# Loading the dense input matrix ahead of the first key piece in a decode step of sliding-window attention and a Mish layer

## The chip, the cores and the metric

The kernel runs on one core of one Trainium2 chip. The metric is the device time of one execution in microseconds. The profile is of one execution; its span, from the first to the last instruction, is a little shorter than the device time.

## The reference

A decode step for a batch of 2, one token each, width 448. The input is normalised once, and two branches are added to it.

```python
xn = layernorm(x)                                   # x: (2, 1, 448)
# attention: 16 query heads, 8 key/value heads, head size 256, last 4096 of 32768 positions
q = (xn @ wq) in 16 heads
p = softmax(q @ k[last 4096].T * 256 ** -0.5)
a = (p @ v[last 4096]) @ wo
# dense: 448 -> 1792 -> 448
h = xn @ w1 + b1
d = (h * tanh(softplus(h))) @ w2
out = x + a + d
```

All inputs are bfloat16. The keys and values of the window are 2 x 8 x 4096 x 256 numbers each, 67 MB together; with the four weight matrices 77.67 MB are read in one execution.

## The kernel before, in words

The work is written out by hand: a manual schedule keeps the instructions of each engine in the order of the program text, and the framework adds the semaphores.

**Units.** The 16 pairs of batch and key head are handled in U = 4 units of J = 4 pairs. A unit's keys come in two pieces, k(u,0) and k(u,1), its values in two pieces, v(u,0) and v(u,1). Each piece is 4096 KB: 128 partitions of 32 KB. A unit's part of the output matrix, wo(u), has 896 KB.

**The ring.** Large loads share three buffers of 32 KB per partition, handed out by `ring` (tag "kv"): wq (two halves of 1792 KB), all key and value pieces, the dense input matrix w1 (1568 KB) and the dense output matrix w2. A load into a used buffer waits until the last reader of the old content is done. All these loads are issued by SyncE, one after the other, so a load that waits holds up those behind it in the program.

**Start.** wq is loaded, then k(0,0) and k(0,1), then the bias b1. Meanwhile the layer norm is computed and the normalised input is turned into `xs`. `project()` makes the queries: 28 matmuls `q_ps` against wq, a copy, transposes, and the spread queries `qd` (its PSUM tiles share one buffer, tag "m"). w1 takes the buffer of wq once the projection has read it.

**Per unit.**
- `turns(u, i)` transposes a key piece on VectorE in 32 x 32 blocks, two instructions a piece (L269 in the profile before).
- `scores(u, i)` writes a mask into PSUM and adds 32 matmuls (L356); ScalarE takes the exponential (L364). After i = 1 VectorE transposes the weights into `p` (L367) and swaps two blocks (`swap`).
- `weigh(u)` sums the weights (`dn`, `rec`).
- `values(u, g)` multiplies a value piece by the weights, 32 matmuls (L402).
- `gather`, `finish`, `relay`, `mix_early` divide by the sum and multiply by wo.

The loop over u issues the loads k(u+1,0), v(u,0), k(u+1,1), v(u,1), wo(u) and then turns and scores of unit u+1 beside the values of unit u.

**The dense branch.** `dense_in()` makes h in PSUM in seven groups, each a bias matmul (L510) and seven matmuls with w1 as the stationary operand (L519). Its PSUM tile `h_ps` uses the same buffer (tag "m") as the projection's last tile `qr_ps`. `mish()` is one exponential on ScalarE (L533) and five small VectorE instructions (L535 to L544). Before, both stand in the text between `turns(0, 1)` and `scores(0, 1)`. The output matrix w2 comes last of all loads, in four parts, and `dense_out` adds its products to `acc`, from which `res` is copied and stored.

Of the kernel before, what the change touches and what calls it, by code (L numbers as in the profile page):

```python
# [17 lines left out]
def kernel(  # L18
# [13 lines left out]
    nc = tc.nc  # L32
    P = 128
# [24 lines left out]
    NS = 7  # L58
    HW = HqDh // 2
    NCH = HW // P  # L60
    F2 = F // 2
# [28 lines left out]
    def ring(name):  # L90
        return kv_pool.tile([P, RK * KE], BF16, tag="kv", name=name)
# [3 lines left out]
    def load_k(u, r):  # L95
        t = ring("k")
        src = kview[u][:, s0:, :].rearrange("j (c t) d -> c j (t d)", c=C)
        nc.sync.dma_start(out=t[:], in_=src[:, :, r * RK * KE : (r + 1) * RK * KE])
        k_t[u, r] = t
# [20 lines left out]
    b1_sb = consts.tile([2, F2], BF16)  # L120
# [4 lines left out]
    for lo in (0, half):  # L125
        nc.sync.dma_start(out=wq[:, lo : lo + half], in_=wq_in[:, lo : lo + half])
    wq_t = [wq[:, i * HW : (i + 1) * HW] for i in range(NS)]
    load_k(0, 0)
    load_k(0, 1)
    nc.sync.dma_start(out=b1_sb[:], in_=B_b1.rearrange("(k f) -> k f", k=2))  # L130

    ident = consts.tile([P, P], BF16)
    make_identity(nc, ident[:])
# [6 lines left out]
        out=halves[:], in_=ident[0:2, 0:2].unsqueeze(2).to_broadcast([2, 2, Bsz])  # L140
# [5 lines left out]
    for k in range(KU):  # L146
        nc.gpsimd.tensor_copy(
            out=hot[:, k, :, :, :, k],
            in_=ident[:].rearrange("p (q y) -> p y q", y=4).unsqueeze(2)
# [11 lines left out]
        out=rstd[:], in_=mv[:, 1:2], func=ACT.Sqrt, bias=eps_t[:], scale=1.0  # L161
# [4 lines left out]
        out=xn_bf[:],  # L166
# [8 lines left out]
        out=parm[:], in_=ident[:].rearrange("p (a o) -> p o a", o=2), axis=AXIS.X, op=ALU.add  # L175
# [3 lines left out]
        out=jm[:],  # L179
        in_=ident[:].rearrange("p (a j h) -> p j a h", j=J, h=rep),  # L180
# [4 lines left out]
        out=jm[:], in0=jm[:], scalar1=-1.0, scalar2=29952.0, op0=ALU.add, op1=ALU.mult  # L185
# [3 lines left out]
        out=mneg[:], in_=jm[:].unsqueeze(1).to_broadcast([P, TH * 8, J])  # L189
    )  # L190
    sel = consts.tile([P, 2, NQ], FP32)
    for x in range(2):
        for w in range(4):
# [4 lines left out]
            else:  # L198
                nc.vector.tensor_tensor(
                    out=sel[:, x, :], in0=sel[:, x, :], in1=src, op=ALU.add  # L200
# [16 lines left out]
    for odd in range(2):  # L217
        for half in range(2):
            o = (half + odd) % 2
            nc.vector.tensor_scalar(  # L220
                out=xs[:, odd::2, half * Bsz : (half + 1) * Bsz],
# [44 lines left out]
    def turns(u, i):  # L266
        t = k_t.pop((u, i))
        for r in range(RK):
            nc.vector.transpose(  # L269
                out=kt[i][:, :, r, :, :],  # L270
                in_=t[:, r * KE : (r + 1) * KE].bitcast(FP32).rearrange(
                    "p (a c j) -> p a c j", c=P // (R * J), j=J
                ),
            )

    spread = {}
    for n in range(2):
        for e in range(2):
# [3 lines left out]
                out=sp[:],  # L282
                in_=ident[:, o : o + 63 : 2].unsqueeze(1).to_broadcast([P, G, 32]),
# [3 lines left out]
    def project():  # L287
        q_ps = ps_m.tile([P, 512], FP32, tag="m", name="q_ps")
        for s in range(NS):
            for u in range(U):  # L290
                nc.tensor.matmul(  # L291
                    q_ps[32 * u : 32 * (u + 1), :],
                    lhsT=xs[:, s, :],
                    rhs=wq_t[s][:, u * 512 : (u + 1) * 512],
                    start=(s == 0),
                    stop=(s == NS - 1),
                    skip_group_check=True,
                )
        q_sb = small.tile([P, 4, P], BF16, tag="vs", name="q_sb", bufs=1)
        nc.scalar.copy(out=q_sb[:].rearrange("p a m -> p (a m)"), in_=q_ps[:])  # L300
        qt_ps = ps_m.tile([P, 4, P], BF16, tag="m", name="qt_ps")
        for a in range(4):
            nc.tensor.transpose(qt_ps[:, a, :], q_sb[:, a, :], ident[:])  # L303
        qT = consts.tile([P, 2, U, Bsz, KU, rep], BF16)
        q_v = qt_ps[:].rearrange("p (h c) (u r) -> p c u r h", c=2, u=U)
        for c in range(2):
            for b in range(Bsz):
                nc.vector.tensor_copy(  # L308
                    out=qT[:, c, :, b, :, :], in_=q_v[:, c, :, b : KU * Bsz : Bsz, :]
                )  # L310
        qr_ps = ps_m.tile([P, 2 * NB, U, NQ], FP32, tag="m", name="qr_ps")
        for n in range(NB):
            for e in range(2):
                nc.tensor.matmul(
                    qr_ps[:, 2 * n + e, :, :].rearrange("p u q -> p (u q)"),
                    lhsT=spread[n % 2, e][:].rearrange("p g a -> p (g a)"),
                    rhs=qT[:, n // 2].rearrange("p u b k h -> p (u b k h)"),
                    start=True,
                    stop=True,
                    skip_group_check=True,  # L320
                )
        for g in range(G):
            rows = slice(g * 32, (g + 1) * 32)
            nc.vector.tensor_copy(
                out=qd[rows, :, :, g, :],
                in_=qr_ps[rows].rearrange("p n u q -> p u n q"),
            )
# [47 lines left out]
    state = {}  # L375
# [119 lines left out]

    act_bf = consts.tile([P, NI, 2, Bsz], BF16)

    def load_w1():
        t = ring("w1")
        nc.sync.dma_start(  # L500
            out=t[:, 0 : NS * F2], in_=B_w1.flatten().rearrange("(p e) -> p e", p=P)
        )
        state["w1"] = t

    def dense_in():
        w1 = state.pop("w1")
        w1_v = w1[:, 0 : NS * F2].rearrange("p (s q i) -> p s i q", s=NS, i=NI)
        h_ps = ps_m.tile([P, NI, 2, Bsz], FP32, tag="m", name="h_ps")
        for i in range(NI):
            nc.tensor.matmul(  # L510
                h_ps[:, i, :, :].rearrange("p k b -> p (k b)"),
                lhsT=b1_sb[:, i::NI],
                rhs=halves[:].rearrange("p k b -> p (k b)"),
                start=True,
                stop=False,
                skip_group_check=True,
            )
            for s in range(NS):
                nc.tensor.matmul(  # L519
                    h_ps[:, i, :, :].rearrange("p k b -> p (k b)"),  # L520
                    lhsT=w1_v[:, s, i, :],
                    rhs=xs[:, s, 0 : 2 * Bsz],
                    start=False,
                    stop=(s == NS - 1),
                    skip_group_check=True,
                )
        state["h"] = h_ps

    def mish():
        h_ps = state.pop("h")  # L530
        shape = [P, NI, 2, Bsz]
        u_sb = consts.tile(shape, FP32, name="u_sb")
        nc.scalar.activation(out=u_sb[:], in_=h_ps[:], func=ACT.Exp)  # L533
        t_sb = consts.tile(shape, FP32, name="t_sb")
        nc.vector.scalar_tensor_tensor(  # L535
            out=t_sb[:], in0=u_sb[:], scalar=2.0, in1=u_sb[:], op0=ALU.add, op1=ALU.mult
        )
        den = consts.tile(shape, FP32, name="den_sb")
        nc.vector.tensor_scalar(
            out=den[:], in0=t_sb[:], scalar1=2.0, scalar2=None, op0=ALU.add  # L540
        )
        nc.vector.reciprocal(out=den[:], in_=den[:])
        nc.vector.tensor_tensor(out=t_sb[:], in0=t_sb[:], in1=den[:], op=ALU.mult)
        nc.vector.tensor_tensor(out=act_bf[:], in0=h_ps[:], in1=t_sb[:], op=ALU.mult)  # L544
# [15 lines left out]
    def dense_out(part):  # L560
        k, lo, hi = w2_parts[part]
        for i in range(lo, hi):
# [2 lines left out]
                act_bf[:, i, k, :], state["w2"][:, at : at + D], stop=(k == 1 and i == NI - 1)  # L565
            )

    load_w1()
    project()
    turns(0, 0)  # L570
    scores(0, 0)
    turns(0, 1)
    dense_in()
    mish()
    scores(0, 1)
    weigh(0)
    for u in range(U - 1):
# [77 lines left out]
```

The softmax here doesn't subtract the row's maximum and nothing guards it: scores larger than these inputs give would overflow.

## Time and profile before

| what | value |
|---|---|
| device time, median of 3 runs | 189.21 us (188.96 to 189.25) |
| span of the profiled execution | 187.2 us |
| TensorE matmul busy | 78.2 us, 42% |
| VectorE busy | 92.7 us, 50% (70.1 us of it the key transposes L269) |
| ScalarE busy | 12.6 us, 7% |
| read from HBM | 77.67 MB, 415 GB/s over the span |
| DMA queue of the loads | 97.0% of 16 engines' span |

The DMA rows of the profile give, for each of 40 slices of the span, the busy share of the core's 16 DMA engines in tenths and the rate. The chain of waits follows the work that ended last back to what released it. The timeline of the SP queue shows when a load is issued; that of an engine shows an instruction group's start, its duration, and in brackets how long the engine was idle before it and what ended that. Engine times are from the span's start.

### The profile page before, as it was taken

Reading aid. Unit: us, or ns where it says so; the run is one execution under the profiler, and the core shown is the slowest. Engines: PE = TensorE matmul, PEld = TensorE weight load, DVE = VectorE, ACT = ScalarE, POOL = GpSimd, SP = SyncE. Lnnn points to the kernel's source line nnn. Section 1 sums busy time; section 2 is a strip of 40 time slices with the busy share of each in tenths; the row PEclk is TensorE's granted clock in tenths of the full one; section 3 lists DMA queues with packets and bytes.
Section 4 is the critical chain, followed back from the end, with each engine's and each line's share of the span. In section 5 each row is a group of like instructions: output and inputs, shape, how many; then the busy total and the mean of one; then the engine's idle time right before and its main releaser. Section 6 shows DMA issues by size and latency. Waiting matters only on the chain.

```text
span 187.2 us, 1951 instructions
## 1 busy us (share of the span) xinstructions
PE 78.2 (42%) x852; PEld 35.3 (19%) x852; DVE 92.7 (50%) x94; ACT 12.6 (7%) x27; POOL 4.9 (3%) x16
## 2 busy tenths in 40 slices
PE   0453014793219200882049002870067004855684
PEld 0211001551003000440012001420022002422283
DVE  6604397984792098038930395048920593040021
ACT  3003000101000100110000100110001000120101
POOL 8100000000000000000000000000000000000000
PEclk9999999958555855698556755897557555996555
DMA  6999999999999999999999999999999999999991
GB/s 218 420 476 441 427 434 387 454 438 448 441 427 420 403 443 404 464 434 448 441 420 424 413 441 417 451 431 448 434 434 420 413 441 427 441 413 416 417 407 42
DMA packets 4195, 77.78 MB, mean 416 GB/s; under 512 B 470, under 2 KB 732, under 8 KB 1628
## 3 DMA queue, kind: packets, MB, share of 16 engines
q1 hardware_dynamic: 4184, 77.67, 97.0%
q8 instruction: 6, 0.10, 0.2%
q14 instruction: 1, 0.01, 0.0%
q10 hardware_dynamic: 4, 0.00, 0.0%
HBM read 77.67 MB, written 0.00 MB: 415 GB/s over the span
## 4 chain that ended last, share of the span: by engine, by line
DMA 62%; PE 17%; DVE 15%; issue 3%; ACT 1%; SPq 0%; DVEq 0%
DMA v<-in_A_v_cache_dram 30%; DMA k<-in_A_k_cache_dram 15%; DVE kt L269 12%; DMA w<-in_B_w_dram 11%; DMA wq<-in_A_wq_dram 6%; PE pv L402 5%; PE sc L356 3%; PE h_ps L519 2%; PE o L420 1%; DVE p L367 1%; PE acc L249 1%; PE dn L380 1%; PE q_ps L291 1%; PE o L435 1%; DVE rec L388 1%
## 5 line engine op out<-in xcount | busy, mean ns | idle before, releaser
L269 DVE STREAM_TRANSPOSE kt<-k 128x4096 f32<-128x4096 f32 x16 | 70.1, 4420 | 33.9 <-DMA k<-in_A_k_cache_dram 33.9
L402 PE MATMUL pv<-v,p 128*32 128x512 bf16 x244 | 25.5, 590 | 72.3 <-DMA v<-in_A_v_cache_dram 72.3
L356 PE MATMUL sc<-kt,qd 128*32 128x512 bf16 x256 | 20.8, 463 | 13.3 <-DVE kt L269 13.3
L402 PEld LDWEIGHTS <-p 128*32 128x32 bf16 x244 | 9.2, 133 | 86.7 <-issue 63.4
L356 PEld LDWEIGHTS <-qd 128*32 128x32 bf16 x256 | 7.4, 109 | 25.5 <-issue 20.5
L364 ACT ACTIVATE ex<-sc 128x512 bf16<-128x512 f32 x8 | 4.8, 597 | 89.6 <-PE sc L356 89.6
L447 DVE TENSOR_TENSOR oT<-o,rec 128x16 bf16<-128x16 f32 x4 | 0.7, 174 | 20.4 <-PE o L420 18.1
L367 DVE STREAM_TRANSPOSE p<-ex 128x512 bf16<-128x512 bf16 x8 | 5.2, 690 | 10.6 <-ACT ex L364 10.6
L388 DVE TENSOR_REDUCE rec<-dn 128x8 f32<-128x512 f32 x4 | 2.8, 692 | 13.5 <-PE dn L380 13.5
L414 ACT COPY vs<-pv 128x512 f32<-128x512 f32 x4 | 2.3, 585 | 56.5 <-PE pv L402 56.5
L420 PE MATMUL o<-sel,vs 128*128 128x8 f32 x32 | 5.2, 289 | 2.1 <-ACT vs L414 2.1
L482 PE MATMUL early<-wo,ox 128*2 128x448 bf16 x24 | 5.0, 352 | 1.9 <-ACT ox L473 1.9
L420 PEld LDWEIGHTS o<-sel,vs 128*128 128x128 f32 x32 | 4.8, 228 | 4.6 <-ACT vs L414 4.6
L380 PE MATMUL dn<-p,ones 128*128 128x512 bf16 x8 | 3.2, 491 | 3.8 <-DVE p L338 3.8
L291 PE MATMUL q_ps<-wq,xs 128*32 128x512 bf16 x28 | 3.8, 623 | 2.3 <-DMA wq<-in_A_wq_dram 1.9
L519 PE MATMUL h_ps<-xs,w 128*128 128x4 bf16 x49 | 3.7, 196 | 1.3 <-DMA w<-in_B_w_dram 1.3
L345 PE MATMUL sc<-mneg,ident 128*128 128x512 bf16 x8 | 4.1, 516 | 0.0
L308 DVE COPY qT<-qt_ps 128x16 bf16<-128x16 bf16 x4 | 0.4, 165 | 7.1 <-PE qt_ps L303 7.1
L212 PE MATMUL xr_ps<-ident,xrows 2*128 2x2 bf16 x7 | 1.0, 181 | 6.7 <-DVE xrows L211 6.7
L519 PEld LDWEIGHTS <-w 128*128 128x128 bf16 x49 | 3.2, 150 | 1.5 <-DMA w<-in_B_w_dram 1.4
L482 PEld LDWEIGHTS <-ox 128*2 128x2 bf16 x24 | 1.8, 83 | 4.1 <-ACT ox L473 2.2
L212 PEld LDWEIGHTS <-xrows 2*128 2x128 bf16 x7 | 0.7, 99 | 6.9 <-DVE xrows L211 6.7
(68 smaller groups left out, 44.9 us busy)
## 6 DMA issues: line engine op xcount, KB each, us to landing
k<-in_A_k_cache_dram SPq DMA_DIRECT2D x8, 4096.0 KB, 27.9
v<-in_A_v_cache_dram SPq DMA_DIRECT2D x7, 4096.0 KB, 21.3
wq<-in_A_wq_dram SPq DMA_DIRECT2D x2, 1792.0 KB, 9.2
wo<-in_A_wo_dram SPq DMA_DIRECT2D x4, 896.0 KB, 18.9
v<-in_A_v_cache_dram SPq DMA_DIRECT2D x1, 2560.0 KB
w<-in_B_w_dram SPq DMA_DIRECT2D x1, 1568.0 KB, 21.2
v<-in_A_v_cache_dram SPq DMA_DIRECT2D x1, 1024.0 KB, 22.0
w<-in_B_w_dram SPq DMA_DIRECT2D x1, 784.0 KB, 22.2
```

The source lines that it names most:

```text
L269: nc.vector.transpose(out=kt[i][:, :, r, :, :], in_=t[:, r * KE : (r + 1) * KE].bitcast(FP32).rearrange("p (a c j) -> p a c j", c=P // (R ...
L291: nc.tensor.matmul(q_ps[32 * u : 32 * (u + 1), :], lhsT=xs[:, s, :], rhs=wq_t[s][:, u * 512 : (u + 1) * 512], start=(s == 0), stop=(s == N ...
L345: nc.tensor.matmul(sc[:].rearrange("p t c m -> p (t c m)"), lhsT=ident[:], rhs=mneg[:].rearrange("p a j -> p (a j)"), start=True, stop=Fal ...
L356: nc.tensor.matmul(sc[32 * w : 32 * (w + 1)].rearrange("p t c m -> p t (c m)"), lhsT=qd[:, u, 2 * n + e, :, :].rearrange("p g q -> p (g q) ...
L364: nc.scalar.activation(out=ex[:, :, :, i, :], in_=sc[:], func=ACT.Exp, scale=scale)
L367: nc.vector.transpose(out=p_all[:, :, h * TH : (h + 1) * TH, :].rearrange("p g t q -> p t g q"), in_=ex[:, h * TH : (h + 1) * TH].rearrang ...
L380: nc.tensor.matmul(dn[:].rearrange("p a q -> p (a q)"), lhsT=ones[:], rhs=p_run[:, i].rearrange("p t q -> p (t q)"), start=(i == 0), stop= ...
L388: nc.vector.tensor_reduce(out=rec[:], in_=dn[:].rearrange("p a q -> p q a"), axis=AXIS.X, op=ALU.add)
L402: nc.tensor.matmul(pv[32 * w : 32 * (w + 1), :, :].rearrange("p x d -> p (x d)"), lhsT=p_run[:, g, 4 * a : 4 * a + 4, :].rearrange("p t q ...
L420: nc.tensor.matmul(po[:, c, :], lhsT=sb[:, x, c::2], rhs=sel[:, x, :], start=(x == 0 and c == 0), stop=(last and x == 1), skip_group_check ...
L482: nc.tensor.matmul(early[:], lhsT=ox[:, i, :], rhs=w[:, i, :], start=False, stop=(u == U - 2 and i == 7),)
L519: nc.tensor.matmul(h_ps[:, i, :, :].rearrange("p k b -> p (k b)"), lhsT=w1_v[:, s, i, :], rhs=xs[:, s, 0 : 2 * Bsz], start=False, stop=(s ...
```

## The change

The load of w1 and that of b1 move ahead of the key pieces. w1 takes a ring buffer of its own at the start instead of that of wq, and so the second key piece, k(0,1), now takes the buffer of wq and waits for the projection. `dense_in()` and `mish()` move from between `turns(0, 1)` and `scores(0, 1)` to right behind `project()`, before the first key piece is transposed. The aim is to have the dense input stage done while the first key piece is still on its way, and out of the way of unit 0's scores.

```diff
@@ start
     wq_t = [wq[:, i * HW : (i + 1) * HW] for i in range(NS)]
+    nc.sync.dma_start(out=b1_sb[:], in_=B_b1.rearrange("(k f) -> k f", k=2))
+    w1 = ring("w1")
+    nc.sync.dma_start(
+        out=w1[:, 0 : NS * F2], in_=B_w1.flatten().rearrange("(p e) -> p e", p=P)
+    )
     load_k(0, 0)
     load_k(0, 1)
-    nc.sync.dma_start(out=b1_sb[:], in_=B_b1.rearrange("(k f) -> k f", k=2))
@@ dense branch
-    def load_w1():
-        t = ring("w1")
-        nc.sync.dma_start(
-            out=t[:, 0 : NS * F2], in_=B_w1.flatten().rearrange("(p e) -> p e", p=P)
-        )
-        state["w1"] = t
-
     def dense_in():
-        w1 = state.pop("w1")
@@ order
-    load_w1()
     project()
+    dense_in()
+    mish()
     turns(0, 0)
     scores(0, 0)
     turns(0, 1)
-    dense_in()
-    mish()
     scores(0, 1)
```

## The prediction

> **What bounds the kernel now.** I read the page first: the DMA rows of its part 2 and the queues of part 3.
>
> ```profile
> DMA  6999999999999999999999999999999999999991
> GB/s 218 420 476 441 427 434 387 454 438 448 441 427 420 403 443 404 464 434 448 441 420 424 413 441 417 451 431 448 434 434 420 413 441 427 441 413 416 417 407 42
> q1 hardware_dynamic: 4184, 77.67, 97.0%
> ```
>
> 38 of 40 slices say 9, while PE is busy 42% and DVE 50%. The digits round, so I next asked for stretches (columns: PE, PEld, DVE, ACT, POOL busy, granted clock, DMA share, GB/s):
>
> ```profile
> 2.00:14.00 12.00, 5.07 (x36) 1.78 (x36) 5.32 (x30) 0.87 (x2) 3.52 (x10) 1.00 1.00 420
> 14.00:36.00 22.00, 6.07 (x56) 2.77 (x54) 15.21 (x11) 2.46 (x3) 0.00 (x0) 1.00 1.00 431
> 36.00:60.00 24.00, 13.54 (x124) 6.59 (x127) 17.07 (x16) 0.79 (x2) 0.00 (x0) 0.59 1.01 435
> 60.00:120.00 60.00, 21.03 (x218) 8.18 (x210) 29.55 (x14) 3.18 (x7) 0.00 (x0) 0.65 1.01 432
> 120.00:182.00 62.00, 30.02 (x339) 13.95 (x339) 24.37 (x22) 4.08 (x11) 0.00 (x0) 0.68 0.99 425
> ```
>
> The DMA share is 0.99 to 1.01 in every stretch from 2 to 182 us. The packet records of the trace are sharper: in each half microsecond from about 2.6 to 181.6 us, 16.0 or more of 16 engines have a packet, and the usual duration of the 1920 packets of 32768 bytes is 1213 ns. So nothing is idle where the change acts, and each byte has a fixed price: 77.67 MB at some 430 GB/s.
>
> The end of the chain of waits shows that the tail hangs on the last transfer:
>
> ```profile
> 182.01 1.98 PE acc L249 x76
> 183.99 0.02 issue
> 184.01 0.57 PE acc L249 x12
> 184.58 0.25 DVE res L621
> ```
>
> The last packets end between 182.3 and 183.9 us, depending on the engine. The 12 matmuls from 184.01 come after the last packet, then the `res` copies, then the store of the output. The change touches none of these.
>
> Last, the order at the start. The timeline of the SP queue shows when a load could be issued, that of DVE when a key piece landed:
>
> ```profile
> 1.65 1.25 SPq L98 DMA_DIRECT2D k<-in_A_k_cache_dram  x2
> 14.19 0.36 SPq L500 DMA_DIRECT2D w<-in_B_w_dram  x1
> 30.73 0.55 SPq L98 DMA_DIRECT2D k<-in_A_k_cache_dram  x1
> 39.61 0.54 SPq L106 DMA_DIRECT2D v<-in_A_v_cache_dram  x1
> 40.45 0.53 SPq L98 DMA_DIRECT2D k<-in_A_k_cache_dram  x1
> 57.45 0.54 SPq L106 DMA_DIRECT2D v<-in_A_v_cache_dram  x1
> ```
>
> ```profile
> 21.93 8.77 DVE L269 STREAM_TRANSPOSE kt<-k 128x4096 f32<-128x4096 f32 x2 [3.76 <-DMA k<-in_A_k_cache_dram]
> 31.66 8.77 DVE L269 STREAM_TRANSPOSE kt<-k 128x4096 f32<-128x4096 f32 x2 [0.95 <-DMA k<-in_A_k_cache_dram]
> 48.70 8.72 DVE L269 STREAM_TRANSPOSE kt<-k 128x4096 f32<-128x4096 f32 x2
> 65.18 8.77 DVE L269 STREAM_TRANSPOSE kt<-k 128x4096 f32<-128x4096 f32 x2 [7.76 <-DMA k<-in_A_k_cache_dram]
> ```
>
> Key piece k(0,0) landed at 21.93 and k(0,1) at 31.66: 9.73 us for 4.19 MB, or 431 GB/s. The dense matrix w1 landed at 35.36 (the chain ends its wait there), 3.70 us later. The third pair of transposes (48.70) waited for earlier DVE work and not for its data. The fourth waited 7.76 us for its data: DVE is ahead again by then.
>
> **What the Trainium skill says.** "DMA: Bandwidth & Descriptors", section Specifications, gives a fabric ceiling of 435 GB/s for a core's 16 DMA engines; the trace's 431 to 435 GB/s agree. Its section on the anatomy of one DMA says that DMA engines do not wait on semaphores: the issuing sequencer waits before dispatch, and the engines merely consume their queues. The SP rows agree: each load is issued when its ring buffer comes free, up to 21 us before its data has landed (w1: 14.19 to 35.36). So a later issue costs time only if the queue has run empty by then. "Runtime: NRT & Kernel Launch", section Instruction fetch mechanics, says that instructions are fetched in 16 KiB blocks; the six packets (0.10 MB) on queue 8 of the page agree.
>
> **The change part by part.** I follow the new order step by step, with durations from before.
>
> 1. *Bytes and packets.* The same loads with the same shapes; only the order differs: wq, b1, w1, k(0,0), k(0,1). DMA work changes by 0. b1 is two rows, 3.5 KB.
>
> 2. *Landings.* wq is still first, so it lands at 12.2 and the projection ends at 14.17 as before. w1 lands 3.70 us after wq, at 15.9. k(0,0) moves from 21.93 to 25.6 and k(0,1) from 31.66 to 35.4, where w1 landed before. The bytes ahead of k(1,0) are the same, so from there nothing is due earlier or later: k(1,0) at 35.4 + 9.7 = 45.1, v(0,0) at 55.3 (its first matmul before), k(1,1) at 65.2.
>
> 3. *dense_in and mish.* `h_ps` uses the PSUM buffer of `qr_ps`, so the first matmul waits for the `qd` copies (16.45 + 1.72 = 18.2); w1 is there. The seven groups took 35.40 to 39.58, 4.2 us, so they end at about 22.4. Queued behind them on PE is `scores(0, 0)`, which cannot go on before the first transposes of k(0,0) end (about 30). The Exp takes 0.19 us; the five DVE steps of mish took 40.35 to 41.59, 1.24 us, and end by 24.0. Queued behind them on DVE are the transposes of k(0,0), whose data comes at 25.6. The table load for Exp (1.28 us, at 14.79 before) now stands ahead of mish's Exp and still lies beside the projection's tail. All hidden: cost 0.
>
> 4. *The new wait on the ring.* Three buffers hold wq, w1 and k(0,0), so k(0,1) waits for wq's last reader: it is issued at 14.2 instead of about 2. The queue then holds the rest of w1 and all of k(0,0), to 25.6: 11 us of work. Behind k(0,1) on SP stand the other loads:
>    - k(1,0) takes w1's buffer after dense_in: 22.4 (30.73 before), needed when k(0,1) lands, 35.4.
>    - v(0,0) takes k(0,0)'s after its transposes: 25.6 + 8.8 = 34.4 (39.61 before), needed at 45.1.
>    - k(1,1) takes k(0,1)'s: 35.4 + 8.8 = 44.2 (40.45 before), needed at 55.3.
>
> 5. *The tightest place.* v(0,1) needs the transposes of k(1,0) to end. After 44.2 PE does the rest of `scores(0, 1)`: 30 matmuls, 3.15 us as at 30.76 before, or 3.9 us at the lower clock seen at 40. Exp, softmax transposes, swap, sums and reciprocal then took from 43.92 to 48.70, 4.8 us. So k(1,0)'s transposes start at 52.2 to 52.9 (48.70 before) and end 8.7 us later, at 60.9 to 61.6. v(0,1) is issued then instead of at 57.45. The queue empties at 65.2. A load's first packet came 1.0 us after its issue at the very start (0.73 to 1.74). That leaves 2.6 to 3.3 us unused.
>
> 6. *After that.* wo(0) and k(2,0) follow v(0,1) at once, as `values(0, 0)` ends near 58.9. The transposes of k(1,1) start with its landing at 65.2, since DVE is free at 61.6, and everything behind is as before. The delay of 3.7 us ends in DVE's wait of 7.76 us.
>
> Sum: 0 on the path. Forecast: 189.2 us.
>
> **The rivals.**
>
> *A bubble in the queue (slower).* Step 5 could be too hopeful: if PE runs slow, or a ring buffer is freed later than I read it, the engines idle, and idle DMA time cannot be won back. For it speaks that v(0,1)'s margin shrinks by 3.5 to 4.2 us. Against it: 2.6 us are still left, and the other margins are 11 to 13 us. If a bubble opened, I would expect 0.5 to 3.7 us (the whole shift): 189.7 to 192.9, most likely about 191.
>
> *A different tail (either side).* The engines do not end together: 182.3 to 183.9. By the packet records, a fetch on queue 8 holds the engine it falls on for 0.87 us, and the packet behind lasts 1.76 us instead of 1.21: 1.4 us together, the size of the spread. PE's instructions change places near the start, so its first fetch may come at another moment, and two fetches on one engine would add up to 1.4 us: 190.6. A better mix ends at most near the mean of the engines, about 0.6 us earlier: 188.6. Against both: the number of instructions is practically the same and the last fetches are far from the change.
>
> *Faster by freed compute.* mish leaves DVE's stretch before the transposes of k(1,0), and PE has dense_in out of its way. If the path were compute, 1.2 us of DVE or up to 4.2 us of PE could go: 188.0 to 185. Against it: the DMA share is 1.00 in that stretch, so earlier compute waits for data.
>
> **How the numbers follow.** No change 0.74; a bubble 0.09; a worse tail 0.05; a better tail 0.09; freed compute 0.03. Hence faster 0.12, same 0.74, slower 0.14. The measured runs of before spread over 0.3 us. The range runs from the best tail, 188.6, to 189.9, which takes in a small bubble or half of a bad tail.
>
> **What would show it right or wrong.** Right: a DMA share near 1.00 in every stretch from 2 to 182; k(0,0)'s transposes near 25.6 and k(0,1)'s near 35.4; dense matmuls from 18 to 22.5; the third pair of transposes at 52 to 53; v(0,1) issued near 61; the fourth pair at 65.2 as before. Step 5 is wrong if a slice near 65 us falls below 0.9 and the first `values` of v(0,1) come after 75. The whole argument is wrong if the time drops by a microsecond with all loads the same, since then the rate of the DMA engines is not fixed.

## The result, and the profile after

The changed kernel takes 190.69 us (median of 6 runs, 190.34 to 191.03) against 189.21 us (188.96 to 189.33). The ratio is 1.008, with a 95% interval from 1.0065 to 1.0095: it is 1.5 us slower. All the work that was moved is hidden, as meant. The time is lost some 40 us later, at the load v(0,1), whose place in the program the change leaves alone.

The DMA rows and the load queue of the page of the changed kernel:

```profile
DMA  6999999999999999999999999999999999999990
GB/s 216 417 426 492 417 420 417 438 431 438 445 445 438 344 419 392 470 445 424 445 424 414 438 431 419 443 438 441 431 445 424 424 407 469 417 421 399 412 389 33
q1 hardware_dynamic: 4184, 77.67, 96.8%
```

The busy row looks as before: 38 slices of 9. The row below it does not. The 14th slice (61.3 to 66.0 us) moved 344 GB/s, the slices beside it 438 and 419. Two stretches asked for on both kernels (columns as in the prediction: PE, PEld, DVE, ACT, POOL busy, clock, DMA share, GB/s) show it apart from the grid of the page. The kernel before:

```profile
44.00:60.00 16.00, 5.65 (x43) 1.80 (x46) 11.70 (x9) 0.52 (x1) 0.00 (x0) 0.59 1.00 432
62.00:70.00 8.00, 0.00 (x0) 0.00 (x0) 4.82 (x2) 0.59 (x1) 0.00 (x0) 0.63 1.02 437
```

The changed kernel:

```profile
44.00:60.00 16.00, 8.49 (x66) 2.92 (x67) 10.78 (x10) 0.60 (x1) 0.00 (x0) 0.72 1.02 442
62.00:70.00 8.00, 3.10 (x30) 1.06 (x23) 5.01 (x2) 0.60 (x1) 0.00 (x0) 0.71 1.00 392
```

Between 62 and 70 us the engines are "busy" for a share of 1.00 and move 392 GB/s instead of 437. Eight microseconds at 45 GB/s less are 0.36 MB, 0.8 us of transfer. What was issued then, by the timeline of the SP queue:

```profile
2.41 20.99 SPq L98 DMA_DIRECT2D k<-in_A_k_cache_dram  x3
35.30 0.54 SPq L106 DMA_DIRECT2D v<-in_A_v_cache_dram  x1
44.82 0.54 SPq L98 DMA_DIRECT2D k<-in_A_k_cache_dram  x1
61.73 0.54 SPq L106 DMA_DIRECT2D v<-in_A_v_cache_dram  x1
62.32 0.60 SPq L112 DMA_DIRECT2D wo<-in_A_wo_dram  x1
63.01 0.56 SPq L98 DMA_DIRECT2D k<-in_A_k_cache_dram  x1
```

The load at 61.73 is v(0,1). Its buffer came free with the third pair of transposes; the timeline of DVE:

```profile
26.50 8.77 DVE L273 STREAM_TRANSPOSE kt<-k 128x4096 f32<-128x4096 f32 x2 [2.13 <-DMA k<-in_A_k_cache_dram]
36.02 8.77 DVE L273 STREAM_TRANSPOSE kt<-k 128x4096 f32<-128x4096 f32 x2 [0.75 <-DMA k<-in_A_k_cache_dram]
52.99 8.72 DVE L273 STREAM_TRANSPOSE kt<-k 128x4096 f32<-128x4096 f32 x2
64.99 8.77 DVE L273 STREAM_TRANSPOSE kt<-k 128x4096 f32<-128x4096 f32 x2 [3.29 <-DMA k<-in_A_k_cache_dram]
```

The fourth pair starts at 64.99, as early as before (65.18): up to the landing of k(1,1) nothing is lost. The next landing is that of v(0,1), and on it waits the next group of values on PE:

```profile
76.25 3.60 PE L406 MATMUL pv<-v,p 128*32 128x512 bf16 x32 [11.16 <-DMA v<-in_A_v_cache_dram]
```

In the kernel before it started at 74.87:

```profile
74.87 3.29 PE L402 MATMUL pv<-v,p 128*32 128x512 bf16 x32 [12.98 <-DMA v<-in_A_v_cache_dram]
```

So it is 1.4 us late. The end carries the same shift (end of the chain of waits):

```profile
183.45 1.95 PE acc L253 x57
185.40 0.01 issue
185.41 0.61 PE acc L253 x12
186.01 0.25 DVE res L616
```

The last 12 matmuls come at 185.41 instead of 184.01, 1.4 us later. The groups of values in between that wait for their data start 1.2 to 1.4 us later as well.

The packet records tell what "busy at 392 GB/s" is. In the table, "engines" counts packets in flight, and the rate spreads each packet over its own duration.

```
us           before: engines, GB/s     after: engines, GB/s
62.5 - 63.0        16.0   425               15.9   429
63.0 - 63.5        16.2   423               15.3   382
63.5 - 64.0        16.0   424               13.7   281
64.0 - 64.5        16.1   425               14.0   284
64.5 - 65.0        16.1   431               15.2   300
65.0 - 65.5        16.0   433               16.1   358
66.0 - 66.5        16.0   433               16.1   398
68.0 - 68.5        16.1   435               16.0   414
69.0 - 69.5        16.1   434               16.0   429
```

The records don't name the engine, but a packet that starts where no other has just ended follows a pause. Four engines have finished k(1,1) at 62.94, 63.23, 63.46 and 63.53, and find nothing behind it. The packets after these pauses start at 63.07, 63.71, 64.62 and 64.77: 1.3 to 3.0 us after the issue of v(0,1) at 61.73. The idle time is small, about 0.2 us in the mean of the 16 engines. The larger part is in long packets: 32 KB packets of v(0,1) last up to 2.6 us instead of 1.21, and it takes until 69 us to be back at full rate. This is how the queue behaved at its very start as well: in the kernel before 183 GB/s from 2.0 to 2.5 us, 363 from 3.0 and 420 from 4.0. So for some of its engines the queue ran dry, and the whole of it ramped up a second time. Why the packets are long, no run here shows.

### The profile page after: what moved, and what is told of

Its sections match the earlier page's. It is cut to its first block, busy times and chain, and to the rows that moved or that the text cites. A ratio compares the mean times of both kernels' runs of the same rounds, so it can differ in the third digit from the quotient of the medians.

```text
span 188.6 us, 1947 instructions
## 1 busy us (share of the span) xinstructions
PE 84.0 (45%) x847; PEld 38.5 (20%) x852; DVE 93.0 (49%) x94; ACT 12.6 (7%) x27; POOL 4.6 (2%) x16
## 3 DMA queue, kind: packets, MB, share of 16 engines
q1 hardware_dynamic: 4184, 77.67, 96.8%
HBM read 77.67 MB, written 0.00 MB: 412 GB/s over the span
## 4 chain that ended last, share of the span: by engine, by line
DMA 61%; DVE 20%; PE 11%; issue 3%; SPq 1%; ACT 1%; another core or an unknown queue 1%; DVEq 0%
DMA v<-in_A_v_cache_dram 29%; DMA k<-in_A_k_cache_dram 26%; DVE kt L273 16%; DMA wq<-in_A_wq_dram 6%; PE pv L406 4%; PE sc L360 3%; DVE p L371 1%; PE acc L253 1%; PE q_ps L295 1%; PE o L424 1%; DVE rec L392 1%; ACT ex L368 1%; SPq L106 1%; PE o L439 0%
## 5 line engine op out<-in xcount | busy, mean ns | idle before, releaser
L273 DVE STREAM_TRANSPOSE kt<-k 128x4096 f32<-128x4096 f32 x16 | 70.0, 4414 | 22.8 <-DMA k<-in_A_k_cache_dram 22.8
L406 PE MATMUL pv<-v,p 128*32 128x512 bf16 x244 | 24.8, 577 | 61.0 <-DMA v<-in_A_v_cache_dram 61.0
L360 PE MATMUL sc<-kt,qd 128*32 128x512 bf16 x256 | 25.6, 537 | 18.4 <-DVE kt L273 18.4
L360 PEld LDWEIGHTS <-qd 128*32 128x32 bf16 x256 | 8.6, 123 | 33.9 <-issue 32.8
L424 PE MATMUL o<-sel,vs 128*128 128x8 f32 x32 | 7.5, 364 | 2.1 <-ACT vs L418 2.1
L424 PEld LDWEIGHTS o<-sel,vs 128*128 128x128 f32 x32 | 7.1, 326 | 5.5 <-ACT vs L418 5.5
L384 PE MATMUL dn<-p,ones 128*128 128x512 bf16 x4 | 2.0, 499 | 4.0 <-DVE p L342 3.8
L143 DVE COPY halves<-ident 2x4 bf16<-2x4 bf16 x1 | 1.9, 1912 | 1.3 <-POOL ident masks.py:199 1.3
## 6 DMA issues: line engine op xcount, KB each, us to landing
v<-in_A_v_cache_dram SPq DMA_DIRECT2D x7, 4096.0 KB, 22.4
```

The costliest lines, as they stand in the source:

```text
L273: nc.vector.transpose(out=kt[i][:, :, r, :, :], in_=t[:, r * KE : (r + 1) * KE].bitcast(FP32).rearrange("p (a c j) -> p a c j", c=P // (R ...
L360: nc.tensor.matmul(sc[32 * w : 32 * (w + 1)].rearrange("p t c m -> p t (c m)"), lhsT=qd[:, u, 2 * n + e, :, :].rearrange("p g q -> p (g q) ...
L406: nc.tensor.matmul(pv[32 * w : 32 * (w + 1), :, :].rearrange("p x d -> p (x d)"), lhsT=p_run[:, g, 4 * a : 4 * a + 4, :].rearrange("p t q ...
L424: nc.tensor.matmul(po[:, c, :], lhsT=sb[:, x, c::2], rhs=sel[:, x, :], start=(x == 0 and c == 0), stop=(last and x == 1), skip_group_check ...
```

## The experiments

Theory: v(0,1) is issued too shortly before the engines run out. Rival 1: loading the dense matrix first costs in itself (a slower start, a wider spread of the engines at the end). Rival 2: the instruction fetch that falls on 63.02 us, 0.05 us ahead of the first long packet, makes the dip; the kernel before had it at 62.03. In the expectations, lead is the time from the issue of v(0,1) to the moment at which the queue has moved as many bytes as were issued ahead of it, by the packet records: 6.04 us before, 1.94 us after. (At that moment, 63.67 us after the change, some engines are past these bytes and others not yet.)

**More bytes ahead of v(0,1).**

```diff
+        if u == 0:
+            load_wo(u)
         load_v(u, 1)
-        load_wo(u)
+        if u > 0:
+            load_wo(u)
```

> The changed kernel with one load moved: wo(0), which needs no ring buffer, is issued before v(0,1) instead of behind it, so 0.92 MB more stand in the queue while v(0,1) waits for the transposes of k(1,0). Theory (a load issued too shortly before the queue runs empty makes the engines drain and ramp up again): v(0,1) is still issued near 61.7, but the bytes ahead of it last 2.1 us longer, so its lead grows from 1.9 to about 4 us; the dip near 63 to 68 us goes away and the time is 189.2 to 189.5. Rival 1 (the early dense load costs time in another way: a slower start, a wider spread of the engines at the end): the time stays 190.4 to 191.0. Rival 2 (the instruction fetch that fell on 63.0 made the dip): the fetch stays where it is, and so do the dip and 190.7.

Measured 189.91 us (188.97 to 190.48, 22 runs), ratio to the kernel before (now 189.05 us in 49 runs) 1.0031 [1.0017, 1.0046]: about half of the loss is gone, and not all as the theory had said. The runs lie between no loss and nearly the full one. In the profiled run (189.78 us) v(0,1) was issued at 62.21 with a lead of 3.56 us, and still engines were idle from 65.07 on; the packets after a pause started at 65.6 to 66.5, 3.4 to 4.3 us after the issue. Bytes ahead help, so rival 1 alone cannot be right; but a lead of 3.6 us was not enough.

**The buffer freed earlier.** In unit 0, the transposes of k(1,0) go ahead of the softmax work on VectorE; loads as in the changed kernel.

```diff
     turns(0, 1)
+    load_k(1, 0)
+    turns(1, 0)
     scores(0, 1)
     weigh(0)
     for u in range(U - 1):
-        load_k(u + 1, 0)
+        if u > 0:
+            load_k(u + 1, 0)
...
-        turns(u + 1, 0)
+        if u > 0:
+            turns(u + 1, 0)
```

> The changed kernel with VectorE's order changed in unit 0: the transposes of k(1,0) go ahead of the softmax transposes, swap and sums of unit 0. Theory: k(1,0) is transposed from about 45.5 to 54.3, v(0,1) is issued near 54.4 with a lead of about 9 us, no dip, 189.2 to 189.5, although values(0,0) starts some 3 us later. Rival 1 (early load costs in another way) and rival 2 (the fetch): 190.4 to 191.0.

Measured 189.04 us (188.92 to 189.53, 14 runs), 0.9994 [0.9982, 1.0005] of the kernel before. The timeline of its SP queue:

```profile
44.70 0.53 SPq L98 DMA_DIRECT2D k<-in_A_k_cache_dram  x1
54.46 0.54 SPq L106 DMA_DIRECT2D v<-in_A_v_cache_dram  x1
```

and its stretches:

```profile
44.00:60.00 16.00, 6.61 (x55) 2.31 (x59) 12.39 (x10) 0.60 (x1) 0.00 (x0) 0.61 1.01 437
62.00:70.00 8.00, 1.78 (x32) 0.73 (x25) 4.85 (x2) 0.60 (x1) 0.00 (x0) 0.93 1.03 440
```

v(0,1) is issued 7.3 us earlier, with a lead of 9.11 us, and the 1.5 us are back. The early load of w1 and the early dense stage are all still there, so they cost nothing: rival 1 is out. The fetch stands at 63.06 here and harms nothing.

**The loss made without the change.** The kernel before, with n extra transposes of 0.69 us on VectorE ahead of those of k(1,0). The loads and their order stay.

```diff
     weigh(0)
+    idle = consts.tile([P, 512], BF16, name="idle")
+    for _ in range(n):
+        nc.vector.transpose(out=idle[:], in_=mneg[:].rearrange("p a j -> p (a j)"))
     for u in range(U - 1):
```

n = 3: 

> The kernel before with three extra transposes of 128x512 bf16 on VectorE (0.69 us each, 2.1 us; their result is not used) ahead of the transposes of k(1,0); loads and their order are those of before. Theory: v(0,1) is issued near 59.5 instead of 57.45, its lead falls from 6.0 to about 4.0 us, which is above the 3.56 us that k(1,0) had in the kernel before without a dip: 189.1 to 189.4. Rival 1: 189.2, as the dense load is not early. Rival 2: 189.2.

n = 4: 

> The kernel before with four extra VectorE transposes (2.8 us) ahead of those of k(1,0). Lead of v(0,1) about 3.3 us, with 32 KB packets in front of it. If the lead in microseconds decides, this is like the wo-first kernel (3.56 us, 189.91): about 189.9, spread widely. If the small packets of wo in front made that one worse, this stays at 189.0 to 189.3.

n = 5: 

> The same with five (3.4 us): lead about 2.6 us. Theory: part of the loss, between the kernel with four and that with six (189.93): 189.2 to 189.9.

n = 6: 

> The kernel before with six such transposes (4.1 us). Theory: v(0,1) is issued near 61.6, its lead is about 1.9 us as in the changed kernel, the same dip appears and the time is 190.3 to 190.9, with the dense load where it was. Rival 1: 189.2, as the dense load is not early. Rival 2 (fetch): it stays near 62.0, where it made no dip in the kernel before: 189.2.

n = 9: 

> The same with nine (6.2 us): v(0,1) is issued near 63.7, when the queue is just empty (lead about -0.2). Theory: the loss grows by about the 2.1 us that the issue is later than with six: 191.5 to 192.5. Rival 1 and rival 2: 189.2.

| n | v(0,1) issued | lead | GB/s, 62 to 70 us | time of the profiled run | median, us | ratio to before [95%] |
|---|---|---|---|---|---|---|
| 0 (before) | 57.45 | 6.04 | 437 | 188.96 | 189.05 (189.03 beside n = 4, 5 and 9) | |
| 3 | 59.65 | 4.09 | 444 | 189.31 | 189.08 (188.99 to 189.32) | 1.0000 [0.9990, 1.0011] |
| 4 | 60.14 | 3.54 | 424 | 189.10 | 189.96 (189.10 to 190.50) | 1.0046 [1.0028, 1.0063] |
| 5 | 60.83 | 2.74 | 440 | 190.16 | 190.17 (189.15 to 191.13) | 1.0054 [1.0036, 1.0073] |
| 6 | 61.82 | 1.89 | 391 | 190.10 | 189.93 (189.37 to 191.08) | 1.0043 [1.0023, 1.0062] |
| 9 | 63.65 | engines already idle | 313 | 191.84 | 191.93 (191.62 to 192.22) | 1.0153 [1.0140, 1.0166] |

The stretches of n = 6 show the changed kernel's dip with the dense load where it always was:

```profile
44.00:60.00 16.00, 4.97 (x37) 1.61 (x37) 14.05 (x15) 0.50 (x1) 0.00 (x0) 0.55 1.02 439
62.00:70.00 8.00, 3.40 (x30) 1.17 (x23) 4.74 (x2) 0.60 (x1) 0.00 (x0) 0.71 0.96 391
```

and n = 9 a real hole, where the share falls too:

```profile
44.00:60.00 16.00, 5.14 (x37) 1.60 (x37) 14.36 (x18) 0.09 (x1) 0.00 (x0) 0.58 1.02 441
62.00:70.00 8.00, 3.51 (x30) 1.23 (x30) 6.11 (x3) 0.60 (x1) 0.00 (x0) 0.79 0.78 313
```

n = 6 and n = 9 make the dip and a loss without the change. 2.1 us of extra VectorE work (n = 3) cost nothing, so that work is not on the path by itself. 2.8 us cost 0.9 us in the median: between n = 3 and n = 4 the medians make a step. From 2.8 to 4.1 us of delay they hardly move, and single runs lie anywhere between no loss and 2 us; at n = 9, where most engines were empty at the issue, the loss is 2.9 us. Two expectations failed: n = 5 is slower than its range (190.17 against 189.2 to 189.9), n = 6 faster (189.93 against 190.3 to 190.9).

The profiles, one for each n, do not show that the dip makes the whole step. In that of n = 4 several engines pause for a moment, and yet the run is as fast as those of before. In that of n = 5 no engine pauses and v(0,1) lands on time, although the run is 1.2 us longer:

```profile
74.69 3.31 PE L402 MATMUL pv<-v,p 128*32 128x512 bf16 x32 [11.93 <-DMA v<-in_A_v_cache_dram]
116.31 3.60 PE L402 MATMUL pv<-v,p 128*32 128x512 bf16 x32 [13.59 <-DMA v<-in_A_v_cache_dram]
185.17 0.57 PE acc L249 x12
```

The kernel before has these at 74.87, 115.77 and 184.01. By the packet records of n = 5 the 16 engines end 0.3 us later in the mean, but the last one 1.15 us later (185.10 against 183.95). This is the prediction's rival of a different tail, in this one run. So what makes the medians of n = 4 and n = 5 is not shown.

Nor does the lead alone decide. In the kernel before, k(1,0) was issued at 30.73 with a lead of only 3.56 us, and no engine paused: 428 to 434 GB/s in each half microsecond from 33 to 38 us. No other load was issued behind it for almost 9 us, while in both kernels two follow v(0,1) within 1.5 us. Whether these delay the packets of v(0,1) was not tested. n = 4 speaks against the guess that the small packets of wo made the first experiment worse: with 32 KB packets in front, its median is just as high.

The gap between the changed kernel's 190.69 us and the 189.93 us of n = 6, at the same lead, is left. Both spread by 0.7 us or more. In the profiles the values of v(0,1) start at 75.44 with n = 6, 0.6 us later than before, and at 76.25 in the changed kernel; n = 6 loses another 0.6 us after that (last matmuls at 185.15).

**The fetch moved away.** 64 small matmuls on TensorE, while it waits for the first key piece, move all its later instructions.

```diff
     mish()
+    pad = ps_m.tile([P, 2 * Bsz], FP32, tag="m", name="pad")
+    for _ in range(64):
+        nc.tensor.matmul(pad[:], lhsT=b1_sb[:, 0::NI], rhs=halves[:]..., start=True, stop=True, ...)
     turns(0, 0)
```

> The changed kernel with 64 small extra matmuls (bias matmul into an unused PSUM tile, about 5 us) on TensorE while it waits for the first key piece. They move every later instruction of TensorE by 128 places, so the instruction fetch that fell on 63.0 comes some 10 us earlier or more; the issue times of the loads stay. Theory (lead of v(0,1) too short): dip and 190.3 to 191.0 as in the changed kernel. Rival 2 (the fetch made the dip, or both together did): no dip, 189.1 to 189.5.

Measured 190.79 us (190.27 to 191.97, 6 runs), 1.0102 [1.0078, 1.0127]. v(0,1) has a lead of 1.84 us. The fetches fall on 49.08 and 84.73 us, none near 63, and the dip is there: 16 engines fall to 10.5, 8.6 and 11.5 in the half microseconds from 63.0. Rival 2 is out. (In the first experiment and with n = 6 and n = 9 a fetch fell into the dip again, at 65.48, 63.23 and 65.24, so these runs could not have told.)

## Why the prediction was wrong, by its own steps

**Steps 1 to 4 held.** The same 77.67 MB. The dense matmuls ran from 18.54 to 22.8 (18.2 to 22.4 forecast), the mish steps ended at 24.4 (24.0), k(1,0) was issued at 22.86, v(0,0) at 35.30 and k(1,1) at 44.82 (22.4, 34.4, 44.2). The first two key pieces landed 0.9 and 0.6 us later than forecast (26.50, 36.02), most of which the later landings don't show. The second experiment proves the part that mattered: the load and the stage as such are free.

**Step 5 failed, in its last subtraction.** The shift itself was sized rightly: transposes of k(1,0) at 52.99 (52.2 to 52.9), v(0,1) issued at 61.73 (60.9 to 61.6). The margin was not 2.6 to 3.3 us but gone, because two of its terms were mis-sized.
- "The queue empties at 65.2" took the landing of k(1,1), as the waiting engine saw it, for the moment at which the queue runs dry. By the packet records of the changed kernel, the first DMA engine has finished k(1,1) at 62.94, the mean engine at 63.5 and the last at 64.56; the transposes that wait for it start at 64.99. A landing is the slowest engine plus the way to the waiting instruction, and 65.2 was up to 2.3 us too late for this purpose.
- "A load's first packet came 1.0 us after its issue" was the fastest engine on an idle queue. The Trainium skill ("DMA: Bandwidth & Descriptors", Specifications) gives about 0.6 us for the first byte of such a load; here it was 1.0 us at the start, 1.3 to 3.0 us in the changed kernel, and up to 4.3 us in the first experiment. The fastest engine says nothing of the others.

The engine that was empty at 62.94 would have needed its next packet 1.2 us after the issue at 61.73; after the pauses, packets came 1.3 to 3.0 us after it. The prediction also had no term for the ramp behind a pause: v(0,1) was finished 0.9 us later in the mean of the engines and 1.4 us later on the last, of which only about 0.2 us is idle time.

**Step 6 held in its order and failed in its sum.** DVE was free at 61.7 and k(1,1)'s transposes came at 64.99, so the delay of the compute chain ended there. But the DMA time lost at 63 us came back nowhere: 1.4 us at 76.25, 1.4 us at the last matmuls.

**The rivals.** The bubble was the right one, with the right place (v(0,1)), and was given 0.09. Its size (189.7 to 192.9, most likely about 191; measured 190.69) came out partly by luck: it was taken from a later issue and idle engines, while the issue came as forecast and most of the loss was slow packets. The faster compute did not come, and the different tail was not needed for the changed kernel: the shift at the end equals that of v(0,1). It did come in the profile of n = 5.

**The sign to look for was half wrong.** The late `values` (76.25, past the 75 named) showed it; "a slice below 0.9" did not, since the busy share stayed at 9 while the rate fell to 344 GB/s.

**What stays open.** Why an issue takes 3 to 4 us to reach some engines when these are at work and 1.3 to 2.3 us when they are idle (n = 9: issued at 63.65, packets from 64.97 to 65.95); why the same kernel loses little or nothing in one run and over 1 us in the next when the lead is 1.9 to 3.5 us; why k(1,0) got by with 3.56 us in the kernel before; and why the changed kernel loses some 0.7 us more than n = 6 at the same lead. No version tried here beats the kernel before: the second experiment, with the queue full throughout, equals it.

## What to carry to other kernels

Where the DMA queue is the bound, an engine off the path still decides when buffers come free: for each load, subtract its issue time from the time the queue would run out of earlier bytes, and watch short leads, not the landing that a waiting engine shows. With these 4 MB loads, the kernel lost nothing when v(0,1) had a lead of 4.1 us, and 0.9 us or more when it had 1.9 us; in between the runs are mixed. Moving a transfer ahead moves every landing behind it, and through the compute between a landing and a release it moves an issue much later. Read the rate beside the busy share: a ramping queue is "busy" and slow.

## What was not expected of the hardware

- The DMA queue, dry for some engines for about 0.2 us in the mean, lost about 0.9 us of transfer in the mean (by the packet records, up to 75 us), and 1.4 us at the landing: 32 KB packets lasted up to 2.6 instead of 1.21 us, and the rate took some 5 us to recover.
- The medians make a step and not a slope: no loss at a lead of 4.1 us, 0.9 us at 3.5 us, no more at 1.9 us. The profiles show the dip behind the loss only at 1.9 us and below.
- 64 extra matmuls on TensorE and 2.1 us of extra VectorE work left the time where it was (190.79 against 190.69, and 189.08 against 189.05).
